# Paired row-tile loads of x and column-half norms in the first phase of a fused adaLN, attention and SwiGLU kernel

## Chip, cores, metric

One core of one Trainium2 chip. The metric is device time in microseconds (us) of one execution. The kernel before takes 1272.08 us (median of the first 3 executions, 1271.87 to 1272.61). The part that the change rewrites is the first 30 us, so everything here is about tenths of a microsecond in 1272.

## The reference, cut to what matters

```
mod = (silu(c) @ w_mod).reshape(1, 6, 1, -1)      # six vectors: sa, ca, ga, sb, cb, gb
h = layernorm(x) * (1 + ca) + sa                  # x: 2048 x 1024, bf16
x = x + ga * attention(h @ wq, k_cache, v_cache) @ wo
h = layernorm(x) * (1 + cb) + sb
x = x + gb * swiglu(h)
```

Before the first attention head can run, the kernel needs for the first 512 rows: x, its norm, its transpose, the scale vector 1 + ca (a product with 2 MB of w_mod), the q projection (wq), and the shift vector sa (2 MB more of w_mod).

## The kernel before

The front of the kernel, with cuts marked by `# ...`. P = 128, D = 1024, DT = 8 column tiles of x, QT = 4 row tiles in the first block of 512 rows. All loads below go through one queue, in program order (SyncE issued them from 0.74 us on: x, then `wm` at 2.60, `wq` at 3.08); the kernel fixes the order on each engine to program order too.

```python
def load_x(tt):
    fetch(out=xt[tt], in_=x2d[tt * P:(tt + 1) * P, :])        # 256 KB
# ...
for tt in range(QT):
    load_x(tt)
for half in range(DH):                 # DH = 2
    load_wm(1, half)                   # 1 MB of w_mod for half of the scale vector
    load_wq8(2 * half)                 # 512 KB
    load_wq8(2 * half + 1)
load_wm(0, 0)                          # 1 MB each for the shift vector
load_wm(0, 1)
# ...
def mod_cols(vec, half, dst, add_one, tiles=(0, 1, 2, 3)):
    for i in tiles:                    # 8 matmuls with one moving column per tile
        for dt in range(DT):
            nc.tensor.matmul(ps[:, i:i + 1], lhsT=wm[:, dt, i * P:(i + 1) * P],
                             rhs=siluc[:, dt:dt + 1], ...)
    nc.vector.tensor_scalar(out=dst[...], in0=ps[...], ...)

# the front: warm(n) issues n matmuls of 512 columns that nobody reads
stats_0(0)                             # VectorE
act_sum(1)                             # ScalarE: sum of tile 1
nc.scalar.copy(out=siluc, in_=sil_ps)
rstd_0(0)
stats_0(2)
act_squares(1)                         # ScalarE: squares of tile 1
warm(3)
xpose_0(0, norm_0(0))                  # norm on GpSimd, 8 transposes on TensorE
rstd_0(1, 1.0 / D)
rstd_0(2)
warm(5)
stats_0(3)
xpose_0(1, norm_0(1))                  # GpSimd
xpose_0(2, ln_norm(2))                 # VectorE
rstd_0(3)
n3 = ln_norm(3)                        # VectorE
mod_cols(1, 0, ca1, True, (0,))        # one scale column
xpose_0(3, n3)
h_scale(0, h0_ps[0][:, 0, :])          # VectorE: (1 + ca) * transposed norm -> hs
nc.scalar.copy(out=h10[:, 4:8, :], in_=h0_ps[1])
mod_cols(1, 0, ca1, True, (1,))
h_scale(1, h0_ps[0][:, 1, :])
mod_cols(1, 0, ca1, True, (2, 3))
# ... then q0(g, dts): q projection of heads 0 to 6 out of hs; later:
q0(2, (6, 7))
sa_mm(0, (2, 3))                       # shift columns
sa_out(0)                              # VectorE copies and casts them
q0(3, (6, 7))
sh_mm(0, range(5))                     # 20 one-column matmuls that read them
# ...
q0(5, (6, 7))
sa_mm(1, (1, 2, 3))
sa_out(1)
q0(H0 - 1, (6,))
q0(H0 - 1, (7,))
sh_mm(1, range(H0))                    # 28 one-column matmuls
```

## Time and profile before

| what | value |
|---|---|
| time | 1272.08 us |
| TensorE busy | 1262.5 of 1270.0 us |
| first q matmul (timeline) | 11.43 us |
| first one-column matmul of the shift vector | 22.26 us |
| first attention matmul (`s_ps`) | 29.91 us |
| TensorE waits after 32 us | none listed |

The page of the kernel before: engine times (busy us, share, instructions), and the chain of work that ended last.

```profile
PE 1262.5 (99%) x7589; PEld 641.1 (50%) x7589; DVE 609.4 (48%) x1332; ACT 335.1 (26%) x440; POOL 4.2 (0%) x15
...
PE 99%; ACT 0%; DMA 0%; POOL 0%; issue 0%; DVE 0%; SPq 0%
```

TensorE is the limit from the first attention matmul to the end. A change of the front is therefore worth what it moves that first `s_ps` matmul, and nothing else. (The chain puts that matmul at 30.07 us, since it counts a matmul from the end of the one before; the timeline has its own start, 29.91. The prediction uses the first, the tables below the second.)

The timeline of the kernel before, from the last norms to the first q matmuls. Columns: start, length in us, engine, line, operation, output and inputs, count; in brackets the idle time of the engine before it and what ended it. POOL is GpSimd, PE TensorE, PEld its weight loads.

```profile
7.83 1.19 POOL L989 TENSOR_SCALAR xn<-x,mv 128x1024 bf16<-128x1024 bf16 x1 [0.58 <-POOL mv L987]
8.64 1.29 DVE L864 TENSOR_SCALAR xn<-x,mv 128x1024 bf16<-128x1024 bf16 x2
9.08 1.07 PE L960 MATMUL h_ps<-ident,xn 128*128 128x128 bf16 x16 [0.23 <-POOL xn L989]
...
10.08 0.35 PE L785 MATMUL mod_ps<-siluc,wm 128*128 128x1 bf16 x8
...
10.29 0.61 PE L960 MATMUL h_ps<-ident,xn 128*128 128x128 bf16 x8
...
10.74 0.74 PE L785 MATMUL mod_ps<-siluc,wm 128*128 128x1 bf16 x24
...
11.43 4.58 PE L1042 MATMUL q_ps<-hs,wq 128*128 128x512 bf16 x20
```

GpSimd's norm of tile 1 ends at 9.02 and the transposes (`h_ps`) start. The first scale column starts at 10.08, with no wait shown.

The waits of TensorE's weight loads in the kernel before, 4 to 32 us (waiter, what it waited for: us in total, times, longest):

```profile
PEld L960 <- POOL xn L989: 2.2, 2, 1.5
...
PEld L1053 <- issue: 0.6, 2, 0.3
PEld L1042 <- DMA wq<-in_A_wq_dram: 0.4, 1, 0.4
...
PEld L785 <- DMA wm<-in_w_mod_dram: 0.3, 1, 0.3
...
PEld L1060 <- DMA wm<-in_w_mod_dram: 0.2, 1, 0.2
```

Three short waits for loads, and two pauses of 0.3 us (L1053) in which TensorE waits for VectorE to copy the shift columns.

### The profile page before, as it was taken

To read this page: it belongs to the slowest core of one execution; us is meant where nothing else is said; L and a number is where in the kernel's file an instruction comes from. 1 tells how busy PE (TensorE), PEld (TensorE's weight loads), DVE (VectorE), ACT (ScalarE), POOL (GpSimd) and SP (SyncE) were. 2 spreads that over 40 slices of the span, in tenths; PEclk is the share of its full clock that TensorE was granted. 3 is DMA by queue.
4 is the path that set the end of the run, shared out by engine and by line. 5 is a ranking of instruction groups with operands and counts; after the bars stand their busy time and mean duration, and the time that the engine had idled before them with its cause. 6 is when DMAs were issued, how large, how long until landed. Compare 5 with 4: busy or idle time off the path is not lost.

```text
span 1270.0 us, 18162 instructions
## 1 busy us (share of the span) xinstructions
PE 1262.5 (99%) x7589; PEld 641.1 (50%) x7589; DVE 609.4 (48%) x1332; ACT 335.1 (26%) x440; POOL 4.2 (0%) x15
## 2 busy tenths in 40 slices
PE   9999999999999999999999999999999999999998
PEld 4555555555555555555554444444444444444444
DVE  5665658785678664677564631311222112221122
ACT  3543334343333433334341111011100111011100
POOL 1000000000000000000000000000000000000000
PEclk9999999999999999999999999999999999999999
DMA  9897657879456655454575479336633565425702
GB/s 290 209 252 180 166 141 168 173 165 219 121 136 175 150 138 153 113 154 113 121 206 143 136 227 247 95 95 212 211 114 105 169 213 181 158 91 168 246 15 71
DMA packets 306891, 204.46 MB, mean 161 GB/s; under 512 B 145649, under 2 KB 303345, under 8 KB 306802
## 3 DMA queue, kind: packets, MB, share of 16 engines
q1 hardware_dynamic: 301890, 199.03, 58.3%
q10 hardware_dynamic: 4912, 4.20, 1.0%
q8 instruction: 61, 1.00, 0.3%
q14 instruction: 28, 0.23, 0.1%
HBM read 165.94 MB, written 4.21 MB: 134 GB/s over the span
## 4 chain that ended last, share of the span: by engine, by line
PE 99%; ACT 0%; DMA 0%; POOL 0%; issue 0%; DVE 0%; SPq 0%
PE gu_ps L1356 30%; PE a_ps L1274 17%; PE q_ps L1199 16%; PE d_ps L1376 15%; PE o_ps L1242 9%; PE s_ps L1210 9%; PE q_ps L1042 1%; DMA x<-in_A_x_dram 0%; PE one_ps L1053 0%; PE mod_ps L785 0%; PE one_ps L1060 0%; PE h_ps L960 0%; ACT junk L981 0%; POOL xn L989 0%; ACT junk L975 0%
## 5 line engine op out<-in xcount | busy, mean ns | idle before, releaser
L1212 ACT ACTIVATE pT<-s_ps 128x1024 bf16<-128x1024 f32 x256 | 249.4, 1020 | 347.4 <-PE s_ps L1210 347.4
L1274 PE MATMUL a_ps<-wo,oT 128*128 128x512 bf16 x1024 | 241.9, 379 | 0.0
L1199 PE MATMUL q_ps<-hT,wq 128*128 128x512 bf16 x960 | 227.1, 379 | 0.0
L1362 DVE TENSOR_TENSOR guT<-gu_ps,sg 128x512 bf16<-128x512 f32 x112 | 77.5, 692 | 286.8 <-ACT sg L1361 286.7
L1356 PE MATMUL gu_ps<-hT,wg 128*128 128x512 bf16 x896 | 211.7, 379 | 0.0
L1361 ACT ACTIVATE sg<-gu_ps 128x512 bf16<-128x512 f32 x112 | 66.9, 597 | 488.7 <-PE gu_ps L1356 480.1
L1376 PE MATMUL d_ps<-wd,guT 128*128 128x512 bf16 (+2 forms) x952 | 194.2, 366 | 0.0
L1356 PE MATMUL gu_ps<-hT,wu 128*128 128x512 bf16 x672 | 163.3, 379 | 0.0
L1274 PEld LDWEIGHTS <-oT 128*128 128x128 bf16 x1024 | 100.2, 98 | 120.6
L946 DVE CAST qT<-q_ps 128x512 bf16<-128x512 f32 x121 | 83.6, 691 | 154.8 <-PE q_ps L1199 154.5
L1199 PEld LDWEIGHTS <-wq 128*128 128x128 bf16 x960 | 93.9, 98 | 113.3
L1376 PEld LDWEIGHTS <-guT 128*128 128x128 bf16 x952 | 90.9, 98 | 102.9
L1242 PEld LDWEIGHTS <-pT 128*128 128x128 bf16 x2048 | 126.6, 98 | 30.2
L1356 PEld LDWEIGHTS <-wg 128*128 128x128 bf16 x896 | 87.6, 98 | 105.5
L1242 PE MATMUL o_ps<-v_sb,pT 128*128 128x129 bf16 x2048 | 137.0, 220 | 0.0
L1210 PE MATMUL s_ps<-qT,kT 128*128 128x512 bf16 x512 | 131.5, 379 | 0.0
L1356 PEld LDWEIGHTS <-wu 128*128 128x128 bf16 x672 | 65.8, 98 | 79.3
L1229 DVE TENSOR_TENSOR oq<-o_ps,rl 128x256 bf16<-128x256 f32 (+2 forms) x256 | 100.6, 419 | 3.9
L1380 DVE TENSOR_TENSOR f<-d_ps,gb_bc 128x512 f32<-128x512 f32 (+2 forms) x34 | 22.4, 660 | 140.8 <-PE d_ps L1376 140.8
L1210 PEld LDWEIGHTS <-kT 128*128 128x128 bf16 x512 | 44.9, 98 | 30.9 <-issue 0.5
L1282 DVE TENSOR_TENSOR acc<-a_ps,acc 128x512 f32<-128x512 f32 x64 | 44.0, 688 | 32.6 <-PE a_ps L1274 32.6
L1356 PE MATMUL gu_ps<-hT,v_sb 128*128 128x512 bf16 x224 | 57.5, 379 | 0.0
(101 smaller groups left out, 426.7 us busy)
## 6 DMA issues: line engine op xcount, KB each, us to landing
wq<-in_A_wq_dram SPq DMA_DIRECT2D x64, 512.0 KB
wo<-in_A_wo_dram SPq DMA_DIRECT2D x64, 512.0 KB
wg<-in_B_w_gate_dram SPq DMA_DIRECT2D x56, 512.0 KB
wd<-in_B_w_down_dram SPq DMA_DIRECT2D x56, 512.0 KB
wu<-in_B_w_up_dram SPq DMA_DIRECT2D x42, 512.0 KB
v_sb<-in_B_w_up_dram SPq DMA_DIRECT2D x14, 512.0 KB
x<-in_A_x_dram SPq DMA_DIRECT2D x16, 256.0 KB
wm<-in_w_mod_dram SPq DMA_DIRECT2D x4, 1024.0 KB
```

The costliest lines, as they stand in the source:

```text
L946: nc.vector.tensor_copy(out=t, in_=q_ps)
L1199: nc.tensor.matmul(q_ps, lhsT=w, rhs=hT[("h1", cc)][:, dt, :], start=(dt == 0), stop=(dt == DT - 1))
L1210: nc.tensor.matmul(s_ps[:, i, :], lhsT=kT[:, kv, j * P:(j + 1) * P], rhs=qT[g], start=True, stop=True)
L1212: nc.scalar.activation(out=p[:, 2 * jj:2 * jj + 2, :], in_=s_ps, func=ACT.Exp, scale=scale)
L1229: nc.vector.tensor_tensor(out=dst, in0=ps[:, s0:s0 + cnt, 0:Dh], in1=sc, op=ALU.mult)
L1242: nc.tensor.matmul(o_slot["ps"][:, s_, :], lhsT=pT[g][:, j, t * P:(t + 1) * P], rhs=v_sb[:, kv, j, 0:VN], start=(j == 0), stop=(j == WT - 1))
L1274: nc.tensor.matmul(a_ps, lhsT=oT[(cc, 2 * q + i)][:, hh % 4, t * P:(t + 1) * P], rhs=wo_tiles[(cc, q, dh, i)][:, hh % 4, :], start=(hh == ...
L1282: nc.vector.tensor_tensor(out=acc[(cc, t)][:, dsl], in0=a_ps, in1=acc[(cc, t)][:, dsl], op=ALU.add)
L1356: nc.tensor.matmul(ps[:, n, :], lhsT=gu_w[(cc, fg, nm, dt // 4)][:, dt % 4, fi * P:(fi + 1) * P], rhs=hT[("h2", cc)][:, dt, :], start=(dt ...
L1361: nc.scalar.activation(out=g, in_=ps[:, 0, :], func=ACT.Silu)
L1362: nc.vector.tensor_tensor(out=guT[(cc, fg)][:, fi, :], in0=ps[:, 1, :], in1=g, op=ALU.mult)
L1376: nc.tensor.matmul(d_ps, lhsT=guT[(cc, f // 4)][:, f % 4, t * P:(t + 1) * P], rhs=wd_tiles[(cc, dh, f // 4)][:, f % 4, c0:c0 + w], start=( ...
```

## The change

The intent: fewer and larger loads of x, so that the weights behind them are issued sooner; the norms split by column halves over VectorE, ScalarE and GpSimd, so that the last norm is ready sooner; all four scale columns (32 matmuls) ahead of the transposes of tiles 1 to 3; and one q matmul moved behind each copy of the shift columns, to cover it. The row tiles after the first four are loaded in pairs too, later. The diff, cut to its core:

```diff
-    xt = [xpool.tile([P, D], BF16, ...) for tt in range(S // P)]
-    def load_x(tt):
-        fetch(out=xt[tt], in_=x2d[tt * P:(tt + 1) * P, :])
+    x2t = [xpool.tile([P, 2, D], BF16, ...) for i in range(S // P // 2)]
+    xt = [x2t[tt // 2][:, tt % 2, :] for tt in range(S // P)]
+    def load_x2(i):                                            # 512 KB
+        fetch(out=x2t[i], in_=x2d[2*i*P:2*(i+1)*P, :].rearrange("(t p) d -> p t d", p=P))
 # ...
-    (the front as printed above)
+    ln_stats(0, mv[0])
+    # ScalarE: sum of tile 1; stats of tile 2 on VectorE; ScalarE: squares of tile 1
+    warm(4)
+    norm_pool(0, m0[:, 4:5], slice(0, D))
+    xpose_0(0, xn0[0], 0)
+    xpose_0(0, xn0[0], 1)
+    rstd_0(mv12)                        # tiles 1 and 2 together
+    ln_stats(3, mv[3])
+    norm_pool(1, m1[:, 4:5], slice(0, 512))
+    # ...
+    norm_dve(2, 0)
+    warm(2)
+    rstd_0(mv[3])
+    norm_act(1, m1[:, 5:6], 1)
+    norm_dve(3, 0)
+    mod_cols(1, 0, ca1, True)           # 32 scale matmuls
+    # ...
+    norm_dve(2, 1)
+    norm_act(3, m3[:, 4:5], 1)
+    xpose_0(1, xn0[1], 0)               # 4 transposes each
+    xpose_0(2, xn0[2], 0)
+    xpose_0(3, xn0[3], 0)
+    xpose_0(1, xn0[1], 1)
+    xpose_0(2, xn0[2], 1)
+    xpose_0(3, xn0[3], 1)
 # ...
-    q0(2, (6, 7))
+    q0(2, (6,))
     sa_mm(0, (2, 3))
     sa_out(0)
+    q0(2, (7,))
 # ...
-    q0(5, (6, 7))
+    q0(5, (6,))
     sa_mm(1, (1, 2, 3))
     sa_out(1)
-    q0(H0 - 1, (6,))
-    q0(H0 - 1, (7,))
+    q0(5, (7,))
+    q0(H0 - 1, (6, 7))
```

More of the change, by code (lines that the diff above doesn't have):

```diff
@@ L686, in fast_path @@
     nc.scalar.dma_start(out=c_r, in_=c_v)
-    xt = [xpool.tile([P, D], BF16, name=f"x{tt}", tag=f"x{tt}") for tt in range(S // P)]
-    def load_x(tt):
-        fetch(out=xt[tt], in_=x2d[tt * P:(tt + 1) * P, :])
+    x2t = [xpool.tile([P, 2, D], BF16, name=f"x{i}", tag=f"x{i}") for i in range(S // P // 2)]
+    xt = [x2t[tt // 2][:, tt % 2, :] for tt in range(S // P)]
+    def load_x2(i):
+        fetch(out=x2t[i], in_=x2d[2 * i * P:2 * (i + 1) * P, :].rearrange("(t p) d -> p t d", p=P))
     wm_tiles = {}
@@ L713, in load_wq8 @@
         wq8.append(t)
-    for tt in range(QT):
-        load_x(tt)
+    for i in range(QT // 2):
+        load_x2(i)
     for half in range(DH):
@@ L848, in ln_stats @@
             return
-        mv = sm.tile([P, 4], FP32, name="mv", tag="mv", bufs=4)
+        mv = sm.tile([P, 8], FP32, name="mv", tag="mv", bufs=4)
         nc.vector.bn_aggr(out=mv[:, 0:2], in_=st)
@@ L956, in fast_path, with xpose_0 @@
     h0_ps = [big("h0_ps", (P, 4, TCW), BF16) for _ in range(2)]
-    def xpose_0(t, n):
-        for dt in range(DT):
-            nc.tensor.transpose(h0_ps[dt // 4][:, dt % 4, t * P:(t + 1) * P],
+    def xpose_0(t, n, half):
+        for i in range(4):
+            dt = 4 * half + i
+            nc.tensor.transpose(h0_ps[half][:, i, t * P:(t + 1) * P],
                                 n[:, dt * P:(dt + 1) * P], ident)
-    def rstd_0(t, sums=1.0):
-        mv = ln[t]
-        nc.scalar.activation(out=mv[:, 2:3], in_=mv[:, 1:2], func=ACT.Ln, bias=eps_t, scale=sums)
-        nc.scalar.activation(out=mv[:, 2:3], in_=mv[:, 2:3], func=ACT.Exp, scale=-0.5)
@@ L968, in stats_0 @@
-    def stats_0(t):
-        mv = ln[t] = sm.tile([P, 4], FP32, name="mv", tag="mv", bufs=4)
-        ln_stats(t, mv)
-    def act_sum(t):
-        mv = ln[t] = sm.tile([P, 4], FP32, name="mv", tag="mv", bufs=4)
-        junk = wk.tile([P, D], BF16, name="junk", tag="junk", bufs=1)
-        nc.scalar.activation(out=junk, in_=xt[t], func=ACT.Identity, accum_out=mv[:, 3:4])
-    def act_squares(t):
-        mv = ln[t]
-        nc.scalar.activation(out=mv[:, 0:1], in_=mv[:, 3:4], func=ACT.Identity, scale=1.0 / D)
-        junk = wk.tile([P, D], BF16, name="junk", tag="junk", bufs=1)
-        nc.scalar.activation(out=junk, in_=xt[t], func=ACT.Square, bias=mv[:, 0:1], scale=-1.0,
-                             accum_out=mv[:, 1:2])
@@ L984, in norm_0 @@
-    def norm_0(t):
-        mv = ln[t]
-        n = wk.tile([P, D], BF16, name="xn", tag="xn", bufs=3)
-        nc.gpsimd.tensor_scalar(out=mv[:, 3:4], in0=mv[:, 0:1], scalar1=-1.0, scalar2=1.0,
-                                op0=ALU.mult, op1=ALU.mult)
-        nc.gpsimd.tensor_scalar(out=n, in0=xt[t], scalar1=mv[:, 3:4], scalar2=mv[:, 2:3],
-                                op0=ALU.add, op1=ALU.mult)
-        return n
-    stats_0(0)
-    act_sum(1)
-    nc.scalar.copy(out=siluc, in_=sil_ps)
@@ L996, in fast_path @@
-    rstd_0(0)
-    stats_0(2)
-    act_squares(1)
-    warm(3)
-    xpose_0(0, norm_0(0))
-    rstd_0(1, 1.0 / D)
-    rstd_0(2)
-    warm(5)
-    stats_0(3)
-    xpose_0(1, norm_0(1))
-    xpose_0(2, ln_norm(2))
-    rstd_0(3)
-    n3 = ln_norm(3)
-    mod_cols(1, 0, ca1, True, (0,))
-    xpose_0(3, n3)
+    m0, m12, m1, m3 = (sm.tile([P, 8], FP32, name="mv", tag="mv", bufs=4) for _ in range(4))
+    mv12 = m12.rearrange("p (a b) -> p a b", a=2)
+    mv = [m0, mv12[:, 0, :], mv12[:, 1, :], m3]
@@ new lines, in fast_path, with rstd_0, xn_tile, norm_dve @@
+    xn0 = {}
+    def rstd_0(m):
+        nc.scalar.activation(out=m[..., 2:3], in_=m[..., 1:2], func=ACT.Ln, bias=eps_t)
+        nc.scalar.activation(out=m[..., 2:3], in_=m[..., 2:3], func=ACT.Exp, scale=-0.5)
+    def xn_tile(t):
+        xn0[t] = wk.tile([P, D], BF16, name="xn", tag="xn", bufs=3)
+    def norm_dve(t, half):
+        sl = slice(half * 512, half * 512 + 512)
+        nc.vector.tensor_scalar(out=xn0[t][:, sl], in0=xt[t][:, sl], scalar1=mv[t][:, 0:1],
+                                scalar2=mv[t][:, 2:3], op0=ALU.subtract, op1=ALU.mult)
@@ new lines, in norm_pool, with norm_act @@
+    def norm_pool(t, minus, sl):
+        nc.gpsimd.tensor_scalar(out=xn0[t][:, sl], in0=xt[t][:, sl], scalar1=minus,
+                                scalar2=mv[t][:, 2:3], op0=ALU.add, op1=ALU.mult)
+    def norm_act(t, minus, half):
+        sl = slice(half * 512, half * 512 + 512)
+        nc.scalar.activation(out=xn0[t][:, sl], in_=xt[t][:, sl], func=ACT.Identity, bias=minus,
+                             scale=mv[t][:, 2:3])
+    ln_stats(0, mv[0])
+    junk = wk.tile([P, D], BF16, name="junk", tag="junk", bufs=1)
@@ new lines, in fast_path @@
+    nc.scalar.activation(out=junk, in_=xt[1], func=ACT.Identity, accum_out=m1[:, 3:4])
+    nc.scalar.activation(out=m1[:, 0:1], in_=m1[:, 3:4], func=ACT.Identity,
+                         scale=1.0 / (32 * D))
+    nc.scalar.copy(out=siluc, in_=sil_ps)
+    nc.gpsimd.tensor_scalar(out=m1[:, 4:5], in0=m1[:, 3:4], scalar1=-1.0 / D, scalar2=1.0,
+                            op0=ALU.mult, op1=ALU.mult)
+    nc.gpsimd.tensor_scalar(out=m0[:, 4:5], in0=mv[0][:, 0:1], scalar1=-1.0, scalar2=1.0,
+                            op0=ALU.mult, op1=ALU.mult)
@@ new lines, in fast_path @@
+    rstd_0(mv[0])
+    ln_stats(2, mv[2])
+    junk = wk.tile([P, D], BF16, name="junk", tag="junk", bufs=1)
+    nc.scalar.activation(out=junk, in_=xt[1], func=ACT.Square, bias=m1[:, 0:1],
+                         scale=-1.0 / 32, accum_out=mv[1][:, 1:2])
+    warm(4)
+    xn_tile(0)
+    norm_pool(0, m0[:, 4:5], slice(0, D))
[3 more added lines that the diff above has]
+    ln_stats(3, mv[3])
+    for t in (1, 2):
+        xn_tile(t)
+    norm_pool(1, m1[:, 4:5], slice(0, 512))
@@ new lines, in fast_path @@
+    nc.gpsimd.tensor_scalar(out=m1[:, 5:6], in0=m1[:, 4:5], scalar1=mv[1][:, 2:3], scalar2=1.0,
+                            op0=ALU.mult, op1=ALU.mult)
+    norm_dve(2, 0)
+    warm(2)
+    rstd_0(mv[3])
+    norm_act(1, m1[:, 5:6], 1)
+    xn_tile(3)
+    norm_dve(3, 0)
+    mod_cols(1, 0, ca1, True)
+    nc.gpsimd.tensor_scalar(out=m3[:, 4:5], in0=mv[3][:, 0:1], scalar1=-1.0, scalar2=mv[3][:, 2:3],
+                            op0=ALU.mult, op1=ALU.mult)
+    norm_dve(2, 1)
+    norm_act(3, m3[:, 4:5], 1)
@@ L1024, in fast_path @@
     nc.scalar.copy(out=h10[:, 4:8, :], in_=h0_ps[1])
-    mod_cols(1, 0, ca1, True, (1,))
     h_scale(1, h0_ps[0][:, 1, :])
-    mod_cols(1, 0, ca1, True, (2, 3))
     h_scale(2, h0_ps[0][:, 2, :])
@@ L1304, in fast_path @@
             at(k + 3, load_gate, vec // 5, gb_bc if vec == 5 else ga_bc)
-    for tt in range(QT, S // P):
+    for tt in range(QT, S // P, 2):
         cc, t = divmod(tt, QT)
-        at(max((cc - 1) * H - 16, 0) + 2 + 2 * t, load_x, tt)
+        at(max((cc - 1) * H - 16, 0) + 2 + 2 * t, load_x2, tt // 2)
     for hg in range(H // 4):
```

## The prediction

> What bounds the kernel. TensorE is busy 1262.5 of 1270.0 us (99%) and the chain that ended last is 99% TensorE. The list of TensorE's waits has nothing after the first phase: from 30 us on the kernel is an unbroken matmul stream whose length the change does not touch. What can change is when that stream starts: the s_ps matmuls of the first head begin at 30.07 us on the chain.
>
> The first phase before, from the timeline and the chain: x tile 0 landed at 3.49, tile 1 at 4.09, tile 2 at 5.7; ScalarE's sum and squares of tile 1 (4.11 to 7.12), GpSimd's norm of tile 1 (7.83 to 9.03), transposes 9.08 to 10.9 with one scale column (8 matmuls) between, the other 24 scale matmuls (0.58 us), q matmuls from 11.43. From there TensorE is nearly gapless to 22.42. It only just follows the loads: weight loads waited 0.41 us for wq at 12.8, 0.28 for the second scale half at 15.8, 0.16 for the first shift half at 22.1. The DMA view shows all engines busy from 2 us on (290 to 400 GB/s). After 22.42 TensorE loses about 0.4 us: twice it waits for the shift columns to be copied and cast by VectorE (24.09 and 27.05; 20 and 28 small matmuls took 0.64 and 0.84 us where 24 ns each, as the 32 scale matmuls' 0.78 us gives, makes 0.48 and 0.67; plus the weight loads' 0.28 us pauses).
>
> The change. (a) Pairing x: two issues fewer on the queue at 0.42 us each, but tile 0 arrives with tile 1, about 0.6 us later (4.1). [...] since engines were already saturated, earlier issue hardly advances the weights. (b) Norms: VectorE's whole-tile norms (0.55 to 0.67 us) become halves (estimate 0.3), GpSimd's tile 1 (1.19) half a tile (0.6), ScalarE takes two halves (estimate 0.75 each from 1.15 for 1024). Walk: stats of tile 3 end at 8.8 to 9.4, last ScalarE half at 10.8 to 11.4, last transposes 11.05 to 11.7, first scaled hs 11.0 to 11.3, q matmuls from 11.2 to 11.7, against 11.43: no certain gain. The 0.58 us of scale matmuls leaves the tail of the path, but ScalarE's last half and h_scale take its place. (c) Any earlier start is eaten at the weight arrivals (12.8, 15.8, 22.1): from the front at most 0.2 to 0.3 us survives. (d) The moved q0 matmuls (0.216 us each) cover the two shift-column waits: about 0.35 us gained, surely on the path.
>
> Sum: 0.35 from (d), 0.05 from the front. Predicted 1271.65 us; 8 in 10 between 1270.9 and 1272.4. Faster by over 2%: 0.5%; within 2%: 99%; slower: 0.5%.
>
> What would show it: first s_ps matmul 0.2 to 0.8 us before 30.07; q matmuls starting near 11.4; small one_ps groups near 24 ns each, without pauses; a longer wait for wm at 15.8 or 22.1 if the front got faster; nothing changed after.
>
> What would make it wrong: wm arriving much earlier or later because of the issue order; TensorE's clock dropping in the idle 8 to 10 us with fewer warm matmuls; [...] ScalarE's chain becoming the last.

The sum comes to 0.35 + 0.05 = 0.4 us gained. That the DMA engines were "saturated" was my reading of their busy share (0.95 to 1.04 between 4 and 8 us, at 267 and 351 GB/s); it did not hold (see below).

## More of the kernel before

Busy time by stretch of the kernel before (length; busy of each engine; granted TensorE clock; DMA share; GB/s):

```profile
4.00:6.00 2.00, 2.00 (x9) 0.72 (x8) 1.27 (x4) 1.82 (x7) 0.29 (x2) 1.00 0.95 267
6.00:8.00 2.00, 0.98 (x11) 0.66 (x11) 1.97 (x5) 1.90 (x6) 1.42 (x3) 1.00 1.04 351
```

From 4 to 6 us the DMA engines are 95% busy, but move only 267 GB/s.

## The result

The changed kernel takes 1271.99 us (median of 6), the kernel before 1272.03 us (6). The ratio is 1.0007, 95% interval 0.9994 to 1.002: the same. Ratios are the mean time of one kernel's fast runs over that of the other's of the same rounds, so not quite the ratio of the medians. The mean is above 1 because two of the six executions were long, 1273.88 and 1276.26 us, at a mean clock of 0.998 and 0.997 instead of 0.999. So a gain of 0.4 us was forecast and 0.04 was measured.

The page of the changed kernel, engine times and chain:

```profile
PE 1262.1 (99%) x7587; PEld 641.2 (50%) x7587; DVE 609.0 (48%) x1331; ACT 336.3 (26%) x440; POOL 4.3 (0%) x17
...
PE 99%; DMA 1%; SPq 0%; DVE 0%; issue 0%
```

Its timeline over the same stretch:

```profile
8.38 0.77 POOL L984 TENSOR_SCALAR xn<-x,mv 128x512 bf16<-128x512 bf16 x1 [0.43 <-ACT mv L973]
8.72 0.58 DVE L980 TENSOR_SCALAR xn<-x,mv 128x512 bf16<-128x512 bf16 x1
9.46 0.42 DVE L980 TENSOR_SCALAR xn<-x,mv 128x512 bf16<-128x512 bf16 x1 [0.16 <-POOL mv L1017]
9.46 1.52 ACT L989 ACTIVATE xn<-x,mv 128x512 bf16<-128x512 bf16 x2
9.68 0.95 PE L786 MATMUL mod_ps<-siluc,wm 128*128 128x1 bf16 x32 [0.62 <-DMA wm<-in_w_mod_dram]
10.50 1.50 PE L962 MATMUL h_ps<-ident,xn 128*128 128x128 bf16 x24
...
11.90 1.89 PE L1065 MATMUL q_ps<-hs,wq 128*128 128x512 bf16 x8
```

The halves of tiles 1 and 2 are ready at 9.15 and 9.30, but TensorE stands idle until 9.68: the 32 scale matmuls are next in its order, and their weights land at 9.64. Then 24 transposes follow, and q starts at 11.90 instead of 11.43. The norms are no longer what TensorE waits for. TensorE's weight-load waits of the changed kernel, 4 to 32 us:

```profile
PEld L962 <- POOL xn L984: 1.6, 1, 1.6
PEld L786 <- DMA wm<-in_w_mod_dram: 1.1, 1, 1.1
...
PEld L1234 <- issue: 0.3, 1, 0.3
```

The later waits for wq and wm and the pauses at the shift columns are gone. The stretch from the first shift columns to the first `s_ps`, in the kernel before and then in the changed one:

```profile
22.26 0.54 PE L1060 MATMUL one_ps<-siluc,wm 128*128 128x1 bf16 x16
...
24.09 0.64 PE L1053 MATMUL one_ps<-sa_bf,wq 128*128 128x1 bf16 x20
...
29.91 1.03 PE L1210 MATMUL s_ps<-qT,kT 128*128 128x512 bf16 x4
```

```profile
22.63 0.54 PE L1083 MATMUL one_ps<-siluc,wm 128*128 128x1 bf16 x16
...
24.29 0.64 PE L1076 MATMUL one_ps<-sa_bf,wq 128*128 128x1 bf16 x20
...
29.95 1.03 PE L1234 MATMUL s_ps<-qT,kT 128*128 128x512 bf16 x4
```

The DMA rate by stretch:

```profile
4.00:6.00 2.00, 2.00 (x7) 0.77 (x7) 1.48 (x4) 1.41 (x4) 0.19 (x1) 1.00 0.99 356
6.00:8.00 2.00, 0.89 (x5) 0.20 (x2) 1.97 (x6) 1.89 (x5) 1.39 (x2) 1.00 1.08 372
```

With two loads of x in place of four, the same engines move 356 GB/s between 4 and 6 us instead of 267. (Over all traces below: 338 to 373 with pairs, 267 to 306 with single loads.) The first scale weights land at 9.64 instead of 10.03, the first shift weights at 21.68 instead of 22.05.

| stage | before | after | gain |
|---|---|---|---|
| first q matmul | 11.43 | 11.90 | -0.47 |
| first shift column matmul | 22.26 | 22.63 | -0.37 |
| from there to the first `s_ps` | 7.65 | 7.32 | +0.33 |
| first `s_ps` | 29.91 | 29.95 | -0.04 |

In these two executions a late front is cancelled by the covered shift columns.

### The profile page after: what moved, and what is told of

Its sections match the earlier page's. It is cut to its first block, busy times and chain, and to the rows that moved or that the text cites. A ratio compares the mean times of both kernels' runs of the same rounds, so it can differ in the third digit from the quotient of the medians.

```text
span 1270.0 us, 18153 instructions
## 1 busy us (share of the span) xinstructions
PE 1262.1 (99%) x7587; PEld 641.2 (50%) x7587; DVE 609.0 (48%) x1331; ACT 336.3 (26%) x440; POOL 4.3 (0%) x17
## 4 chain that ended last, share of the span: by engine, by line
PE 99%; DMA 1%; SPq 0%; DVE 0%; issue 0%
PE gu_ps L1380 30%; PE a_ps L1298 17%; PE q_ps L1223 16%; PE d_ps L1400 15%; PE o_ps L1266 9%; PE s_ps L1234 9%; PE q_ps L1065 1%; DMA wm<-in_w_mod_dram 1%; PE mod_ps L786 0%; PE one_ps L1083 0%; PE h_ps L962 0%; PE one_ps L1076 0%; SPq L664 0%; PE q_ps L1129 0%; DVE f L1404 0%
```

## The experiments

Theory 1: the front loses because every transpose of tiles 1 to 3 stands behind the scale columns, which wait for `wm`; the moved q matmuls gain 0.33 us behind it. Rivals: the paired x makes the norms late; or the loads bound everything, and the moves are worth nothing. All runs had 5 rounds. Kernels share the executions of the kernel before (9): its medians are 1272.01 (e1 to e4), 1271.99 (after_again, e5, e6, e8) and 1272.02 (e9, e10, e2_again, e11, on another chip than the first two). Positions are from one traced execution each, and the landing of `wm` differs between executions by some tenths (9.64 and 9.29 in the two traces of the changed kernel), so single positions are read against that landing. Where an expectation compares `s_ps` with 30.07 or 30.11, it means the chain's position, 0.16 us above the table's.

| run | wm landed | first q | q minus landing | shift column to s_ps | s_ps | median us | range |
|---|---|---|---|---|---|---|---|
| before | 10.03 | 11.43 | 1.40 | 7.65 | 29.91 | 1272.03 | 1271.87 to 1272.61 |
| after | 9.64 | 11.90 | 2.26 | 7.32 | 29.95 | 1271.99 | 1271.8 to 1276.26 |
| e1_q0_only | 10.42 | 11.82 | 1.40 | 7.53 | 30.33 | 1272.04 | 1271.46 to 1272.28 |
| e2_cols_behind | 9.50 | 11.40 | 1.90 | 7.32 | 29.44 | 1271.51 | 1271.32 to 1271.62 |
| e3_x_single | 10.12 | 12.78 | 2.66 | 7.32 | 32.04 | 1273.04 | 1271.95 to 1274.17 |
| e4_no_q0_move | 9.32 | 11.59 | 2.27 | 7.65 | 29.96 | 1271.96 | 1271.42 to 1276.18 |
| after_again | 9.29 | 11.56 | 2.27 | 7.32 | 29.61 | 1272.07 | 1271.51 to 1272.4 |
| e5_no_warm | 9.34 | 12.77 | 3.43 | 7.32 | 31.81 | 1273.5 | 1273.12 to 1273.73 |
| e6_more_warm | 8.95 | 11.66 | 2.71 | 7.31 | 29.70 | 1271.7 | 1271.58 to 1272.13 |
| e8_cols_warm | 8.88 | 11.41 | 2.53 | 7.32 | 29.46 | 1271.66 | 1271.53 to 1274.61 |
| e9_pairs_q0 | 9.15 | 12.14 | 2.99 | 7.32 | 30.31 | 1272.21 | 1272.19 to 1272.29 |
| e10_pairs_only | 8.99 | 12.11 | 3.12 | 7.65 | 30.60 | 1272.65 | 1272.57 to 1273.23 |
| e2_again | 9.34 | 11.47 | 2.13 | 7.32 | 29.52 | 1271.78 | 1271.57 to 1274.19 |
| e11_before_warm42 | 10.14 | 11.54 | 1.40 | 7.79 | 30.15 | 1272.12 | 1271.98 to 1272.58 |

### e1_q0_only: the moved q matmuls alone

The kernel before with the last part of the diff only:

```diff
-    q0(2, (6, 7))
+    q0(2, (6,))
     sa_mm(0, (2, 3)); sa_out(0)
+    q0(2, (7,))
-    q0(5, (6, 7))
+    q0(5, (6,))
     sa_mm(1, (1, 2, 3)); sa_out(1)
-    q0(H0 - 1, (6,)); q0(H0 - 1, (7,))
+    q0(5, (7,)); q0(H0 - 1, (6, 7))
```

> The kernel before with only the moved q0 matmuls (behind the two copies of the shift columns). Theory 1 (the move gains about 0.35 us, and in the full change the front gives it away again): the first s_ps matmul at 29.7 to 29.8 us against 30.07 before, the 20 and 28 small matmuls after the copies at about 0.48 and 0.67 us instead of 0.64 and 0.84, time 1271.6 to 1271.8, that is 0.3 to 0.4 us under the kernel before. Rival (the weight loads bound this stage, so the move gains nothing): s_ps at 30.0 to 30.1 and the same time within 0.1 us.

Measured: 1272.04 against 1272.01, no gain in the median. The forecast failed. The traced execution (1272.28, the slowest of the five) fits the rival: in it the loads were late (`wm` for the first scale half 10.42, for the second shift half 25.75), and the stretch from the shift columns to `s_ps` took 7.53 us, with a gap of 0.2 us before the shift matmuls at 25.80, just behind that load. In this execution covering the copies is worth 0.12 us of the 0.33. That late loads explain the median too is not shown: two of the five (1271.46 and 1271.63) lie below the kernel before.

### e2_cols_behind: the scale columns behind eight transposes

The changed kernel with one line moved:

```diff
-    mod_cols(1, 0, ca1, True)
     # ...
     xpose_0(1, xn0[1], 0)
     xpose_0(2, xn0[2], 0)
+    mod_cols(1, 0, ca1, True)
     xpose_0(3, xn0[3], 0)
```

> The changed kernel with the 32 scale matmuls moved behind the half-0 transposes of tiles 1 and 2. Theory 1 (the front lost 0.5 us because all 24 transposes stand behind the scale columns, which wait for wm until 9.64): 0.45 us of transposes run while wm is still on its way, q matmuls start at 11.4 to 11.5 instead of 11.9, first s_ps at 29.6 to 29.75 instead of 30.11, time 0.35 to 0.5 us under the changed kernel. Rival 1 (the paired x makes the norms late): transposes wait for the norms instead, q matmuls still start at 11.8 or later, no gain. Rival 2 (later weights catch up): q starts early, but waits for wm at about 15.5 and 22 appear and s_ps stays above 29.9.

Measured: 1271.51, 0.50 us under the kernel before, all five executions within 0.3 us. Timeline of e2:

```profile
8.33 0.77 POOL L984 TENSOR_SCALAR xn<-x,mv 128x512 bf16<-128x512 bf16 x1 [0.44 <-ACT mv L973]
...
9.15 0.62 PE L962 MATMUL h_ps<-ident,xn 128*128 128x128 bf16 x8 [0.15 <-POOL xn L984]
9.61 0.94 PE L786 MATMUL mod_ps<-siluc,wm 128*128 128x1 bf16 x32
10.41 1.05 PE L962 MATMUL h_ps<-ident,xn 128*128 128x128 bf16 x16
11.40 2.32 PE L1065 MATMUL q_ps<-hs,wq 128*128 128x512 bf16 x9
```

Eight transposes now run while `wm` is on its way, q starts at 11.40, 1.90 us behind the landing instead of 2.26, and no wait for a load follows. This is what theory 1 said, and the rival that the later loads would catch up is out for this front. The norms, though, become the limit again. The scale columns start at 9.61, without a gap behind the eight transposes, and these waited for GpSimd's half norm of tile 1, which ends at 9.10. So 1.90 us is no constant of this order: in e8 and e2_again, which share it, `wm` lands at 8.88 and 9.34, and q still starts at 11.41 and 11.47 (lines below).

### e3_x_single: x one tile at a time under the new front

```diff
-        fetch(out=x2t[i], in_=x2d[2*i*P:2*(i+1)*P, :].rearrange(...))
+        for tt in (2 * i, 2 * i + 1):
+            fetch(out=xt[tt], in_=x2d[tt * P:(tt + 1) * P, :])
```

> The changed kernel with x loaded one row tile at a time again (order and all else as changed). Theory 1 (wm's landing holds the front, not the norms): stats start near 3.5 instead of 4.5 us, but the scale matmuls still wait for wm to 9.6 or later, q matmuls start at 11.9 to 12.2, s_ps at 30.1 or up to 0.3 later, time the same within 0.2 us. Rival 1 (paired x makes the norms and so the front late): q matmuls start at 11.4 to 11.5, time 0.3 us or more below the changed kernel.

Measured: 1273.04, but not for either theory's reason. `wm` landed at 10.12, and three of five executions (1273.92, 1274.17, 1273.04) lie 1 us or more above the other two. The traced one is the first of these, and shows why. Busy time by stretch of e3 (TensorE only; then granted clock, DMA share, GB/s), and its timeline:

```profile
4.97:8.39 3.42, 2.62 (x17) 1.00 1.04 341
8.39:11.80 3.41, 1.64 (x48) 1.00 1.02 341
11.80:15.21 3.41, 3.19 (x18) 0.50 1.09 366
```

```profile
10.17 0.95 PE L787 MATMUL mod_ps<-siluc,wm 128*128 128x1 bf16 x32 [1.77 <-DMA wm<-in_w_mod_dram]
10.98 2.01 PE L963 MATMUL h_ps<-ident,xn 128*128 128x128 bf16 x24
12.78 0.63 PE L1066 MATMUL q_ps<-hs,wq 128*128 128x512 bf16 x1
```

From 11.80 to 15.21 us, 3.41 us, the granted clock is 0.50; in the 3.41 us before that it is 1.00, and TensorE is busy for 1.64 us, with almost nothing but one-column matmuls and transposes, and idle for 1.77 us in one piece. The execution took 1273.92 us, about 1.9 more than the two undisturbed ones. That the little work in the one stretch brought the lower clock of the next was my reading (the "clock theory" of the later runs); this trace alone does not show the cause. The two undisturbed executions, 1271.95 and 1272.06, are within 0.2 us of the changed kernel, as theory 1 said. Under this front rival 1 is out: TensorE waits for `wm`, not for a norm.

### e4_no_q0_move: the changed kernel without the moved q matmuls

The last part of the diff is taken back in the changed kernel (the edit of e1 reversed).

> The changed kernel without the q0 moves. Theory 1 (their gain of 0.3 to 0.35 us is there and hides the loss of the front): first s_ps at 30.4 to 30.5 us, time 0.3 us over the changed kernel and over the kernel before. Rival (the stage is bound by the weight loads, the moves are worth nothing): s_ps at 30.1, the same time within 0.1 us. For both: if single runs of 2 to 4 us more with a lower mean clock come in the changed front and never in the kernel before, the changed front itself, not the q0 moves, brings them, and e4 may show them too.

Measured: 1271.96 with one execution of 1276.18. In the trace the mechanism is as expected: 7.65 us again from the shift columns to `s_ps`. In the time, the 0.3 us do not show: `wm` happened to land at 9.32 in the traced execution, which is as much again as the moves give. As a measurement of the time this run is inconclusive; e9 and e10 settle it below, under the old front. Its long execution came without the moved q matmuls, so these are not what brings the long ones.

### after_again, e5_no_warm, e6_more_warm: the long executions

The changed kernel again without an edit; then, with no warm-up matmuls in the front (e5), and with more (e6):

```diff
-    warm(4)            # e5: none        e6: warm(7)
     norm_pool(0, ...)
     # ...
-    warm(2)            # e5: none        e6: warm(4)
```

> The changed kernel once more, unedited, to count how often it has the long executions (2 of 6 so far, 1273.9 and 1276.3, against none of 15 of the kernel before), beside the warm variants on the same chip. If the clock drop seen in e3's trace (half speed from 11.80 to 15.21 us) is their cause: 1 to 3 of 5 executions at 1273 or more with a mean clock of 0.997 or 0.998, the rest at 1271.6 to 1272.1. Rival (a chance disturbance of that chip): none.

> The changed kernel without its two groups of 4 and 2 warm-up matmuls in the front. Clock theory (TensorE sees too little work between 8 and 12 us in some executions and is halved for about 3.4 us at a time): clearly more long executions, 3 to 5 of 5 at 1273 to 1277, and a trace with half-speed matmuls after 11 us. Rival (the long executions have nothing to do with TensorE's activity): as the changed kernel, at most 2 of 5, and q matmuls at the same place.

> The changed kernel with 7 and 4 warm-up matmuls in place of 4 and 2, all in time where TensorE waits (6.9 to 8.0 and 8.9 to 9.6 us). Clock theory: no execution over 1272.7, median 1271.7 to 1272.1 as the undisturbed executions of the changed kernel. Rival: long executions in 1 or 2 of 5 as before. If the warm-up matmuls run into the transposes, q starts up to 0.3 us later and the median rises by as much.

Measured: after_again had no long execution in five (the expectation of 1 to 3 failed); with the first six that is 2 of 11. In e5 all five took 1273.12 to 1273.73, as the clock theory said, and its trace has a clock of 0.50. Stretches of e5, all engines, then clock, DMA share and GB/s:

```profile
4.53:7.94 3.41, 0.93 (x4) 0.20 (x2) 3.21 (x7) 3.05 (x9) 1.39 (x3) 1.00 1.02 355
7.94:11.36 3.42, 3.01 (x51) 2.75 (x52) 2.41 (x7) 2.51 (x6) 1.50 (x4) 0.50 1.03 371
11.36:14.77 3.41, 3.19 (x20) 2.17 (x19) 2.86 (x6) 1.76 (x1) 0.00 (x0) 0.50 1.09 363
```

After 3.41 us with 0.93 us of TensorE work (512-column warm-up matmuls of the group before the front) the clock is 0.50 over two stretches, from 7.94 to 14.77 us. In the first of them TensorE was busy for 3.01 us, with transposes and one-column matmuls, and the clock was 0.50 in the second as well. So the traced execution without the front's warm-up matmuls has the lower clock, as the theory said; how little work it takes was not measured. e6 had no long execution, median 1271.7. Its warm-up matmuls, though, ran until the scale columns at 9.45, while `wm` had landed at 8.95: they are not free when the load is early. (e5's mean clock was low in only two of its five executions. The other three, with 0.999, 0.999 and 1.0, have the mean clock of the undisturbed ones, so what made them 1.1 to 1.5 us longer than the kernel before stays open.)

### e8_cols_warm and e2_again: can the better order be made safe?

e8 is e2 with `warm(7)` and `warm(3)`; e2_again is e2 unedited.

> e2 (scale columns behind the transposes of two tiles) with 7 and 3 warm-up matmuls instead of 4 and 2, meant as the version without the long executions. Theory 1 with the clock theory: 1271.4 to 1271.6 in all five, q matmuls at wm's landing plus 1.9 us (about 11.4), s_ps at 29.6 to 29.7. If the added warm-up matmuls get in the way: q at 11.6 or later and 0.2 us more.

> e2 once more, to see whether its freedom from long executions holds (0 of 5; e8, with more warm-up matmuls, had 1 of 5). Median 1271.4 to 1271.7 if e2's gain is real. [...] if e2's order had cured them, none.

Measured: e8 1271.66, one of five at 1274.61; e2_again 1271.78, one of five at 1274.19, both long ones at a clock of 0.998. The start of the scale columns and of q, first in e8, then in e2_again:

```profile
9.63 0.94 PE L786 MATMUL mod_ps<-siluc,wm 128*128 128x1 bf16 x32
...
11.41 4.48 PE L1065 MATMUL q_ps<-hs,wq 128*128 128x512 bf16 x19
```

```profile
9.69 0.94 PE L786 MATMUL mod_ps<-siluc,wm 128*128 128x1 bf16 x32
...
11.47 4.48 PE L1065 MATMUL q_ps<-hs,wq 128*128 128x512 bf16 x19
```

The medians are 0.33, 0.24 and, in e2, 0.50 us under the kernel before, and in the three traces q starts at 11.40 to 11.47. How much of the time the order alone brings is less sure: no call held e2 beside the changed kernel, and e6, which keeps the order of the change, had a median of 1271.7 in the call in which e8 had 1271.66. Neither variant is free of long executions, so that part of e8's forecast failed.

### e9_pairs_q0 and e10_pairs_only: the paired x under the old front

The kernel before with paired loads of x (the first part of the diff), and with (e9) or without (e10) the moved q matmuls.

> The kernel before with its own front (whole-tile norms, first scale column between the transposes, 3 and 5 warm-up matmuls) plus only the paired x and the moved q0 matmuls. Theory now: q starts at the landing of the first scale weights plus the TensorE work left behind it (1.40 us in the old order, 1.90 in e2, 2.27 in the change), and the pairs bring that landing from 10.0 to about 9.5. So q at 11.0 to 11.3, s_ps at 29.2 to 29.6, time 1271.1 to 1271.6, none over 1273 because the warm-up matmuls are those of before. Rival (the pairs make the old norms late by 0.4 to 0.7 us, which is what the new norms are for): transposes wait for norms, q at 11.6 or later, time 1271.8 or more.

> The kernel before with only the paired x. Theory: scale weights land 0.4 us earlier, q at 11.0 to 11.3, the second and third waits for wm stay away, and the shift-column waits remain (first small one_ps group to s_ps 7.65 us instead of 7.32): s_ps at 29.6 to 29.9, time 1271.5 to 1271.8. Rival (norms late): q at 11.6 or later, time 1272.0 or more.

Measured: 1272.21 and 1272.65. My theory of that moment (q starts at the landing of `wm` plus a fixed rest) failed, and the rival holds. Timeline of e10:

```profile
8.70 1.20 POOL L990 TENSOR_SCALAR xn<-x,mv 128x1024 bf16<-128x1024 bf16 x1 [0.59 <-ACT mv L967]
9.96 1.07 PE L961 MATMUL h_ps<-ident,xn 128*128 128x128 bf16 x16 [0.24 <-POOL xn L990]
10.86 0.34 PE L786 MATMUL mod_ps<-siluc,wm 128*128 128x1 bf16 x8
11.51 0.74 PE L786 MATMUL mod_ps<-siluc,wm 128*128 128x1 bf16 x24
```

`wm` had landed at 8.99, but GpSimd's norm of tile 1 ends at 9.90 instead of 9.02, since tiles 0 and 1 arrive together at 4.49 instead of 3.47 and 4.09. The transposes wait for it and q starts at 12.11. So the pairs alone cost 0.63 us (1272.65 against 1272.02). With the moved q matmuls they cost 0.19, so here the moves gain 0.44 us, with no overlap of the two ranges; the traces show 0.33 of it, 7.32 us instead of 7.65. The shift weights now land at 21.43 (e10) and 21.55 (e9) instead of 22.05, and no wait for a load is left in that stretch.

### e11_before_warm42: fewer warm-up matmuls alone

The kernel before with `warm(4)` and `warm(2)` in place of `warm(3)` and `warm(5)`.

> The kernel before with the change's number of warm-up matmuls (4 and 2 in place of 3 and 5), nothing else. If the fewer warm-up matmuls alone bring the long executions: 1 to 3 of 5 at 1273 or more with a mean clock of 0.997 to 0.998, the rest at 1271.8 to 1272.3. If it takes the later front too (TensorE waiting with no work until wm lands): none, all at 1271.8 to 1272.6.

Measured: 1272.12, no long execution in five. The smaller number of warm-up matmuls alone was not seen to bring them. The count over all calls, an execution being long when it is 1.5 us or more above the fastest of its kernel in that call: 7 of 41 for the kernels with the new front and some warm-up matmuls (after and after_again 2 of 11, e2 and e2_again 1 of 10, e3 2, e4 1, e6 0, e8 1 of 5 each), 0 of 53 for those with the old front (33 of the kernel before, 20 of e1, e9, e10, e11). All seven have a mean clock of 0.997 or 0.998. (By that count e3's third, 1273.04, 1.1 us above its fastest, is not one.) That the lower clock (0.50 from 11.80 to 15.21 us) is the cause is shown for e3's traced execution. For the other six, which were not traced, it is an inference from their clock. One of them (e2_again) came on another chip, so they are not a matter of one chip. What brings the lower clock in them is open.

## Why the prediction was wrong

The range held the median, but a gain of 0.4 us was forecast and 0.04 us came.

- Right: the kernel is bound by TensorE after 30 us and nothing later changes. In the traced executions the first `s_ps` came 0.04 us later; the median fell by 0.04. Both are within the spread of single executions.
- Right: the moved q matmuls, "about 0.35 us gained, surely on the path". The stretch from the shift columns to `s_ps` fell from 7.65 to 7.32 us. "Surely" was too much: under single loads of x (e1) no gain showed in the median, and in the trace late weights ate part of it; under paired loads (e9 against e10) it is worth 0.44 us.
- Right in part: the stats of tile 3 end at 8.80 (forecast 8.8 to 9.4) and ScalarE's last half at 10.98 (10.8 to 11.4).
- **The step that failed is the term of the front: "0.05 from the front", with q from 11.2 to 11.7.** It measured -0.47 us (q at 11.90), of which -0.37 was left at the shift columns. (In after_again `wm` landed at 9.29 and q started at 11.56, a loss of 0.13: the landing, not the norms, sets it.) I walked the norms and put the transposes behind the last norm, at 11.05 to 11.7. I wrote that "the 0.58 us of scale matmuls leaves the tail of the path", though in TensorE's order all 32 of them now stood ahead of 24 transposes and behind a 1 MB load. The true sum is 9.64 (landing) + 0.95 + 1.36 from the chain of waits to the end of the transposes, that is about 12.0, with every norm ready in time. In three traces of this order (after, e4, after_again; e3 and e5 have the clock at 0.50, and in e6 warm-up matmuls hold the columns until 9.45) q starts 2.26 to 2.27 us behind the landing, wherever that lies. e2 moves eight of the transposes back ahead of the columns, and q starts 0.36 us closer to the landing, at a median of 1271.51.
- Wrong, in the other direction: "since engines were already saturated, earlier issue hardly advances the weights". A DMA share of 95% was read as saturation, and the rate as 290 to 400 GB/s, though the same view has 218 GB/s between 4.0 and 4.8 us. The paired loads raised the rate from 267 to 356 GB/s between 4 and 6 us, and the shift weights came 0.4 us earlier. In all ten traces with pairs the scale weights land at 8.88 to 9.64, in all four with single loads at 10.03 to 10.42, whichever the front. Why two loads move more than four in that stretch was not tested.
- Wrong: "any earlier start is eaten at the weight arrivals". With paired loads none of these waits is left, in the changed kernel or in e2.
- Not forecast: that the pairs by themselves cost 0.63 us through the old norms (e10). The new norms are what makes the pairs bearable. In medians: pairs +0.63, moved q matmuls -0.44, new norms with the new column order -0.1 to -0.2 (1271.99 and 1272.07 against 1272.21, from different calls), sum about zero.
- Named as a risk and true in some executions: the clock around the idle stretch between 8 and 10 us (0.50 from 11.80 to 15.21 us in e3's trace, from 7.94 to 14.77 in e5's; 1.00 from 2 to 18 us in the trace of the changed kernel itself). It does not move the median of the changed kernel, but, as far as the mean clock of the long executions tells (0.997 or 0.998), it moves the mean.

The version that came out best is e2: 1271.51 and 1271.78 against 1272.01 and 1272.02, with one long execution in ten. Counting that one, its mean is 1271.85 over its ten executions, against 1272.08 for the 18 of the kernel before in the same two calls: a lead of 0.2 us.

## What to carry to other kernels

When work is reordered on an engine that runs it in program order, as TensorE did here (idle until 9.68 us, with norms for its transposes ready at 9.15), list what stands behind each instruction that waits for a load, and add up all of it from the landing of that load. A start is the later of that sum and the sum of the data chain, and shortening only one of them gains only up to the other: in e2, e8 and e2_again `wm` landed between 8.88 and 9.50, and q started at 11.40 to 11.47 in all three. Where a change thins out TensorE's work, look at the single executions and their clock and not at the median alone: the changed kernel had the median of the kernel before (1271.99 against 1272.03), with 2 long executions in 11 at a mean clock of 0.998 and 0.997.

## Measured beside the main question

- In the changed kernel VectorE's half tile, started at 8.72 while GpSimd's half norm ran from 8.38 to 9.15, took 0.58 us, and its two later halves 0.40 and 0.42. In e3 a half started at 8.56, with GpSimd's half norm running from 7.99 to 8.76, took 0.36. What makes the difference was not tested.
- On GpSimd a norm of 512 columns took 0.77 us and one of 1024 took 1.19 to 1.20, so halving the columns saved only a third. A straight line through the two leaves about 0.35 us that does not shrink (an estimate from these two times; VectorE worked beside the half tile).
